# A list scheduler with transfer durations from a trace, later estimates for TensorE, and a second block handled by halves

## The chip, the core and the metric

The kernel runs on one core of a Trainium2 chip. A core has engines with instruction streams of their own: TensorE (PE; matmuls, and PEld for its weight loads), VectorE (DVE), ScalarE (ACT), GpSimd (POOL) and SyncE (SP). SP issues most of the transfers; sixteen DMA engines carry them. Each engine works off its own stream strictly in the order in which it was written, and waits on semaphores for the others. The metric is the device time of one execution in microseconds (us).

## What is computed

An attention with a decaying complex state, followed by a mixture of experts over all tokens:

```python
# B, H, S, D = 4, 8, 768, 48; per step t:
S_re, S_im = (ar * S_re - ai * S_im) + kv, ar * S_im + ai * S_re   # kv = k_t v_t^T, a normalised to |a| < 1
y[:, :, t] = q_t . S_re
...
x = y as (3072, 384)
P = exp(x @ w_gate - max), then 8 rounds of normalising rows and columns
out = sum over 8 experts e of P[:, e] * (relu(x @ w1[e]) @ w2[e])   # w1[e]: 384x1024, w2[e]: 1024x384
```

Matmuls are done to fp32 accuracy with split operands: each operand is a high part (one rounding) and a low part (the rest), and a product takes three matmuls.

## The kernel before

**Two phases.** Phase 1 (`phase1`) does the attention for 12 blocks of 256 tokens, and beside it experts 0 and 1 on the blocks whose x is done. Phase 2 (`phase2a`, `phase2b`) does experts 2 to 7 on units of 768 tokens with a fast matrix multiplication scheme of 15 products; it ends with the mixing by P. The change touches phase 1 alone.

**A block i in phase 1** has 256 tokens in two chunks c of 128. Its steps, with the method that adds them:

- `load(i)`: SP brings qk (768 KB) and v (512 KB).
- `norm(i)`: z (the complex decay a, 768 KB) is brought, then a chain that goes to and fro between ScalarE (Square L403, root L405, Square L406 and L409) and VectorE (L404, L407, L408, L410, L411, two products L413).
- `scan(i)`: the running product of a inside the block, all on VectorE (L440 to L445).
- `post(i)`: reciprocal magnitudes (ScalarE L485, L487, L488; VectorE L486, L491 to L493), then kh = k scaled (L495) and z times q (L497).
- `attention(i)`, per chunk: 6 transfers "ks" and 6 "qs" turn kh and z to head-major tiles (L531, about 64 KB each, all issued by SP); TensorE transposes keys (L539), forms scores (L549, needs ks and qs), state update U (L560) and outputs yp (L574). VectorE masks the scores (L552) and updates the state (L603 to L608). ScalarE copies keys (L542), a few columns of qs (L578 to L580) and evicts yp as xh (L596); VectorE makes the low part xl (L597). x then goes to DRAM (L614).
- `logits(i)`: x times the gate (L627, L628, L632 on TensorE; L635, L637 on ScalarE).
- `experts(i - 1)`: for each of 2 experts and 8 slices, first matmul (L264 to L266), relus on ScalarE (L270, hh and hf), low part on VectorE (L274), second matmul (L282 to L284), at the end evictions (L290) and a transfer (L305).

`weights` prepares experts 0 and 1 at the start: a load (L217 whole, L237 in thirds), the high part on ScalarE (L220, L242), the low part through TensorE with an identity and a negated identity (L203, L204) and back by ScalarE (L207).

**Who sets the order.** None of this is put in order by hand. Each step calls `Plan.add(engine, us, run, reads, writes, rank, ...)`; `Plan.order` then plays a list scheduler: it keeps a clock per engine (PE, DVE, ACT, SP), takes the engine that can start first, and of that engine's ready operations the one with the lowest rank. The result is one fixed order of instructions for each engine. An operation is ready when all that it depends on has ended, plus a reach from one engine to the other:

```python
REACH = {("PE", "ACT"): 0.20, ("PE", "DVE"): 0.20, ("DVE", "DVE"): 0.11, ("ACT", "PE"): 0.35, ("DVE", "PE"): 0.35, ...}
...
wait = 0.12 if e == "DVE" else 0.0     # VectorE may hold on this long for a better rank
...
pipe = max(t + 0.3, pipe) + kb / 330.0     # a transfer: queued behind the others,
end = max(pipe, t + kb / 210.0) + 1.6      # and with a time of its own by its size
```

So the times in `add` are estimates that decide only the order. On the chip an engine whose next instruction has to wait stands still, even if a later one could run.

At the last step of the attention the plan is cut: expert operations that come after it (`rest`) are issued in phase 2a, beside the loading of phase 2's X tiles (L686 to L715).

**Ranks.** Block i's scan and post have ranks from 1000 i. The norm of block i + 1 has a rank just below the scan of block i (from i + 1 = 2 on), with its last three VectorE operations 900 later. Attention steps have large negative ranks (first when ready), expert matmuls 10 n.

Of the kernel before, what the change touches and what calls it, by code (L numbers as in the profile page):

```python
# [18 lines left out]
CH = 128  # L19
# [36 lines left out]


class Plan:
    REACH = {("PE", "ACT"): 0.20, ("PE", "DVE"): 0.20, ("DVE", "DVE"): 0.11, ("ACT", "PE"): 0.35, ("DVE", "PE"): 0.35, ("ACT", "ACT"): 0.12, ("PE", "PE"): 0.0, ("SP", "PE"): 0.3}

    def __init__(self):
        self.ops, self.wrote, self.read = [], {}, {}

    def add(self, eng, us, run, reads=(), writes=(), rank=0, kb=0, late=0.0, after=()):
        deps = set(after)
        for r in reads:
            deps |= self.wrote.get(r, set())
        for w in writes:
            deps |= self.wrote.get(w, set()) | self.read.get(w, set())
        k = len(self.ops)  # L70
        self.ops.append((eng, us, run, rank, kb, late, sorted(deps)))
        for w in writes:
            self.wrote[w], self.read[w] = {k}, set()
        for r in reads:
            if r not in writes:
                self.read.setdefault(r, set()).add(k)
        return k

    def order(self):
# [10 lines left out]
        pipe = 0.0  # L90
        for k in range(n):
            if not left[k]:
                queue[self.ops[k][0]].append(k)
        out = []
        while any(queue.values()):
            best = None
            for e, q in queue.items():
                if q:
                    t = max(free[e], min(ready[k] for k in q))
                    if best is None or t < best[0]:  # L100
                        best = (t, e)
            t, e = best
            wait = 0.12 if e == "DVE" else 0.0
            k = min((k for k in queue[e] if ready[k] <= t + wait), key=lambda k: (self.ops[k][3], k))
            queue[e].remove(k)
            eng, us, run, rank, kb, late, deps = self.ops[k]
            t = max(t, ready[k])
            self.start[k] = t
            free[e] = t + us
            end = t + us  # L110
            if kb:
                pipe = max(t + 0.3, pipe) + kb / 330.0
                end = max(pipe, t + kb / 210.0) + 1.6
            self.end[k] = end
            out.append(k)
            for u in users[k]:
                r = end + (0.1 if kb else self.REACH.get((e, self.ops[u][0]), 0.15))
                ready[u] = max(ready[u], r)
                left[u] -= 1
                if not left[u]:  # L120
                    queue[self.ops[u][0]].append(u)
        assert len(out) == n
        return out


class Net:
# [63 lines left out]
    def weights(self, wx):  # L190
# [18 lines left out]
        for n in range(RING):  # L209
            e, f = divmod(n, NF)  # L210
            s = ("wx", n % 4)

            def load(n=n, e=e, f=f):
                assert len(raws) == n
                self.wt[e, f] = (self.wp if n < WIDE else self.wy).tile([128, 2, 2 * C], F32R, tag="w", name=f"w{e}_{f}")
                raws[n] = wx.tile([128, 2 * C], F32, tag="w", name=f"wr{e}_{f}")
                nc.sync.dma_start(raws[n], self.w[e, f])  # L217

            job("SP", 0.45, load, (), [s], -1.9e6 + 1e4 * n, kb=384)
            job("ACT", 0.74, lambda n=n, e=e, f=f: A.activation(self.wt[e, f][:, 0, :], raws[n], AF.Copy), [s], [("wh", n)], 10 * n)  # L220
            for j in range(2):
                cs = slice(j * C, j * C + C)
                piece_w(lambda n=n, cs=cs: raws[n][:, cs], lambda e=e, f=f: self.wt[e, f], cs, banks[turn % 4], [s, ("wh", n)], [("wl", n, j)], 10 * n + j, 0.65)
                turn += 1
            self.wd[e, f] = ([("wh", n), ("wl", n, 0)], [("wh", n), ("wl", n, 1)])
        thirds, k = {}, 0
        for n in range(RING, NF + N1):
            e, f = divmod(n, NF)
            for j in range(3):
# [15 lines left out]
                job("SP", 0.45, load, (), [s], -1.7e6 + k, kb=128)  # L245
# [8 lines left out]
    def experts(self, i):  # L254
# [37 lines left out]
        for e in range(2):  # L292
            for f in range(NF):
                n = (2 * i + e) * NF + f
                p = self.ph[n % 2][:, :SUB]
                b, q = ("ph", n % 2), (self.nthird + n) % (LAG + 1)
                w1, w2 = self.wd[e, f]
                job("PE", 1.07, lambda e=e, f=f, p=p: first(e, f, p), xr + w1, [b], 10 * n, late=0.0)
                job("ACT", 0.28, lambda e=e, f=f, p=p: relu("hh", e, f, p), [b], [("hh", q)], -1e6 + 2 * n)
                job("ACT", 0.28, lambda e=e, f=f, p=p: relu("hf", e, f, p), [b], [("hf", n % 2)], -1e6 + 2 * n + 1)  # L300
                job("DVE", 0.345, lambda e=e, f=f: low(e, f), [("hh", q), ("hf", n % 2)], [("hl", q)], -1e6 + n)
                job("PE", 1.05, lambda e=e, f=f: second(e, f), [("hh", q), ("hl", q)] + w2, [("po", 0), ("po", 1)], 10 * n + 5)
            for k in range(NCH):
                job("ACT", 0.5, lambda e=e, k=k: evict(e, k), [("po", k)], [("yst", k)], -8e5)
                job("SP", 0.45, lambda e=e, k=k: nc.sync.dma_start(self.ye_d[e][i * NCH + k], Y[e, k]), [("yst", k)], (), 0, kb=192)  # L305
        self.expert.update(range(n0, len(self.plan.ops)))

    def phase1(self, c1, ca):
# [65 lines left out]

    def load(self, i):
        nc, job, qk, vt = self.nc, self.plan.add, self.qk, self.vt
        job("SP", 0.45, lambda: nc.sync.dma_start(qk, self.aqk[i, :, 2:4]), (), [("qk", c) for c in range(NCH)], -1.85e6 if i == 0 else -1e5, kb=768)
        job("SP", 0.45, lambda: nc.sync.dma_start(vt, self.v[i]), (), ["v"], -1.65e6 if i == 0 else -1e5, kb=512)

    def norm(self, i):  # L380
        nc, V, A, job = self.nc, self.nc.vector, self.nc.scalar, self.plan.add
# [3 lines left out]
        R = 1000 * i  # L385
        if i == 0:
            for a in range(2):
                job("SP" if a else "ACT", 0.45, lambda a=a: (nc.sync if a else nc.scalar).dma_start(zt[:, a, :, :CH], self.aqk[0, :, a]), (), [("z", s, a, c) for c in range(NCH)], -2e6, kb=384)
        else:
            job("SP", 0.45, lambda: nc.sync.dma_start(zt[:, :, :, :CH], self.aqk[i, :, 0:2]), (), zn, -1.82e6 if i == 1 else -1e5, kb=768)  # L390
        for ps in ([[0], [1]] if i == 0 else [[0, 1]]):
            def nm(*t):
                return [(*t, c) for c in ps]
# [4 lines left out]
            zs = [("z", s, a, c) for a in range(2) for c in ps]  # L398
            X, Y, Z, Q = nm("tx"), nm("ty"), nm("tz"), nm("sq")
            f0, f1 = (i, ns + i) if ps[0] == 0 else (2 * ns + ns * NCT * NCH, 2 * ns + ns * NCT * NCH + 1)  # L400
            r = R - 1001 + ps[0] / 2 if i > 1 else R - 300 + 20 * ps[0]
            u = 900 if i > 1 else 0
            job("ACT", n / 522 + 0.1, lambda z=z, sq=sq, f0=f0: A.activation(sq, z, AF.Square, accum_out=fl[:, f0:f0 + 1]), zs, Q, r - 5e5)  # L403
            job("DVE", n / 960 + 0.105, lambda sq=sq, x=x: V.scalar_tensor_tensor(x, sq[:, 0], 1e-20, sq[:, 1], ALU.max, ALU.add), Q, X, r)  # L404
            job("ACT", n / 1045, lambda x=x, y=y: A.activation(y, x, AF.Abs_reciprocal_sqrt), X, Y, r + 1 - 5e5)  # L405
# [64 lines left out]
    def post(self, i):  # L470
# [1 line left out]
        s, fl, ns = i % 2, self.fl, self.N // SUB  # L472
        zt, G = self.zt[s], NCT * NCH
        xs, gs = (t.rearrange("p a g t -> p (a g t)").rearrange("p (g t) -> p g t", t=CH) for t in (self.ta, self.tb))
        for ps in ([[0], [1]] if i == 0 else [[0, 1]]):
            n = 3 * CH * len(ps)
            z, kh, qk = self.cut(zt[:, :, :, :CH], ps), self.cut(self.kh, ps), self.cut(self.qk, ps)
            x, g = (t[:, 3 * ps[0]:3 * ps[0] + 3 * len(ps)] for t in (xs, gs))
# [20 lines left out]
    def attention(self, i):  # L499
# [17 lines left out]
        def chunk(c):  # L517
# [9 lines left out]
            for t, dst, src, w in (("ks", ks, kh, CH), ("qs", qs, zt, CH + 1)):  # L527
                for a in range(2):
                    for ct in range(NCT):
                        p = 64 * a + 16 * ct  # L530
                        job("SP", 0.6, lambda p=p, dst=dst, src=src, w=w, a=a, ct=ct, c=c: nc.sync.dma_start(dst[p:p + 16, :, :w], src[:, a, ct * NCH + c, :w]),  # L531
                            [("kh", a, c)] if t == "ks" else [("z", s, a, c), ("ze", s, c)], [(t, ib, a, ct)], -3e6 + 20 * q + (6 if t == "qs" else 0) + 3 * a + ct, kb=170)
# [79 lines left out]
            chunk(c)  # L612
        for a, t in enumerate(("xh", "xl")):
            job("SP", 0.62, lambda a=a: nc.sync.dma_start(self.x_d[i // NS][:, i % NS, a], x_of()[a].bitcast(F32).rearrange("p c (j t) -> p c j t", t=CH)),  # L614
                [(t, s, c) for c in range(NCH)], (), -2e5, kb=384)

    def logits(self, i):
        nc, A, job = self.nc, self.nc.scalar, self.plan.add
# [737 lines left out]
```

## Time and profile before

| | us |
|---|---|
| median of 3 runs | 1784.88 (1783.31 to 1785.74) |
| profiled execution, its time | 1789.63 |
| profiled execution, its span | 1787.9 |
| TensorE busy in it | 1712.7 |
| VectorE busy | 1302.5 |
| ScalarE busy | 763.4 |
| granted TensorE clock, mean | 0.990 |

The page sums up one profiled execution. Rows by stage (a stretch of the span) give for each engine the busy time and the count of instructions, PE, PEld, DVE, ACT and POOL in this order, then the granted TensorE clock as a share of full speed, the mean busy share of the 16 DMA engines, and GB/s. Rows of waits read: who waited, for whom, us in total, times, longest. Rows in order of time begin with the start and the duration in us; in brackets stands the engine's idle time before, and who ended it. Rows of transfers give KB each and the median us from issue to landing.

### The profile page before, as it was taken

How to read it: one execution, taken by the hardware profiler on the slowest of the kernel's cores; microseconds unless marked ns; L12 is line 12 of the kernel's file. 1: busy time of each engine (PE TensorE's matmuls, PEld its weight loads, DVE VectorE, ACT ScalarE, POOL GpSimd, SP SyncE). 2: the span in 40 equal slices, each digit the busy share in tenths (PEclk: the TensorE clock that was granted, in tenths of full speed). 3: DMA queues.
4: the chain of work that ended last, by engine and by line, in shares of the span. 5: the costliest groups of instructions: out<-in, count | busy, mean ns of one | idle time of the engine just before them, and what ended most of it. 6: DMA issues, size and time to landing. Idle time of an engine off the chain costs nothing.

```text
span 1787.9 us, 32828 instructions
## 1 busy us (share of the span) xinstructions
PE 1712.7 (96%) x12696; PEld 1661.9 (93%) x12696; DVE 1302.5 (73%) x2892; ACT 763.4 (43%) x1694; POOL 6.4 (0%) x15
## 2 busy tenths in 40 slices
PE   6889999999999999999999999999999999999998
PEld 3878898888889898999999999999999999999998
DVE  7888888888888558999985567665566766556564
ACT  7544444444444354655553333333433333333332
POOL 1000000000000000000000000000000000000000
PEclk9999998999999999999999999999999999999999
DMA  6343332333333665787887465667555557455551
GB/s 205 106 119 119 111 95 67 114 109 106 116 118 93 194 235 198 261 292 271 292 305 272 176 234 189 248 226 252 224 187 220 202 218 261 183 223 179 224 227 45
DMA packets 180388, 335.90 MB, mean 188 GB/s; under 512 B 15104, under 2 KB 139776, under 8 KB 180224
## 3 DMA queue, kind: packets, MB, share of 16 engines
q1 hardware_dynamic: 179440, 333.33, 53.7%
q8 instruction: 102, 1.67, 0.4%
q14 instruction: 62, 0.51, 0.1%
q10 hardware_dynamic: 784, 0.39, 0.1%
HBM read 233.71 MB, written 81.00 MB: 176 GB/s over the span
## 4 chain that ended last, share of the span: by engine, by line


## 5 line engine op out<-in xcount | busy, mean ns | idle before, releaser
L1094 ACT ACTIVATE hh<-s 128x384 fp32r<-128x384 f32 x384 | 202.0, 526 | 424.5 <-DVE s L1090 383.9
L1090 DVE TENSOR_TENSOR s<-s,A 128x384 f32<-128x384 f32 x316 | 174.4, 552 | 145.2 <-PE A L1076 139.2
L1000 PE MATMUL po<-w_d,hl 128*128 128x384 f32 x768 | 256.6, 334 | 0.0
L999 PE MATMUL po<-w_d,hh 128*128 128x384 f32 x768 | 256.6, 334 | 0.0
L998 PE MATMUL po<-w_d,hh 128*128 128x384 f32 x768 | 256.6, 334 | 0.0
L1101 DVE SCALAR_TENSOR_TENSOR hl<-s,hh 128x384 fp32r<-128x384 f32 x384 | 211.8, 551 | 6.2
L264 PE MATMUL ph<-xh,w 128*128 128x256 f32 x576 | 166.1, 288 | 7.0 <-ACT hf L270 6.9
L265 PE MATMUL ph<-xl,w 128*128 128x256 f32 x576 | 163.0, 283 | 0.0
L266 PE MATMUL ph<-xh,w 128*128 128x256 f32 x576 | 163.0, 283 | 0.0
L270 ACT ACTIVATE hh<-ph 128x256 fp32r<-128x256 f32 x192 | 73.2, 381 | 176.6 <-PE ph L266 176.0
L1087 ACT ACTIVATE s<-B 128x384 f32<-128x384 f32 x192 | 94.3, 491 | 119.3 <-PE B L1076 115.8
L998 PEld LDWEIGHTS po<-w_d,hh 128*128 128x128 f32 x768 | 144.2, 188 | 0.0
L1000 PEld LDWEIGHTS po<-w_d,hl 128*128 128x128 f32 x768 | 144.1, 188 | 0.0
L999 PEld LDWEIGHTS po<-w_d,hh 128*128 128x128 f32 x768 | 144.1, 188 | 0.0
L1090 DVE TENSOR_TENSOR s<-s,B 128x384 f32<-128x384 f32 x189 | 104.0, 550 | 54.4 <-PE B L1076 52.0
L282 PE MATMUL po<-w,hh 128*128 128x384 f32 x384 | 134.6, 350 | 0.0
L284 PE MATMUL po<-w,hl 128*128 128x384 f32 x384 | 130.2, 339 | 2.4 <-DVE hl L274 2.3
L283 PE MATMUL po<-w,hh 128*128 128x384 f32 x384 | 129.4, 337 | 0.0
L1000 PE MATMUL po<-w_c,hl 128*128 128x384 f32 x384 | 128.5, 335 | 0.0
L999 PE MATMUL po<-w_c,hh 128*128 128x384 f32 x384 | 128.5, 335 | 0.0
L998 PE MATMUL po<-w_c,hh 128*128 128x384 f32 x384 | 128.5, 335 | 0.0
L1109 DVE TENSOR_TENSOR s<-s,B 128x384 f32<-128x384 f32 x64 | 35.5, 554 | 117.1 <-PE B L1076 116.1
(236 smaller groups left out, 4063.0 us busy)
## 6 DMA issues: line engine op xcount, KB each, us to landing
w_d<-w_d SPq DMA_DIRECT2D x64, 768.0 KB, 6.8
w_a<-w_d SPq DMA_DIRECT2D x48, 768.0 KB, 4.3
w_b<-w_d SPq DMA_DIRECT2D x48, 768.0 KB, 5.7
w_c<-w_d SPq DMA_DIRECT2D x48, 768.0 KB, 6.1
raw<-in_w_dram SPq DMA_DIRECT2D x32, 576.0 KB, 5.4
w_d<-w_a SPq DMA_DIRECT2D x16, 768.0 KB, 3.2
w_d<-w_b SPq DMA_DIRECT2D x16, 768.0 KB, 4.7
w_d<-w_c SPq DMA_DIRECT2D x16, 768.0 KB, 6.2
```

The lines of the kernel that those rows point to most:

```text
L264: nc.tensor.matmul(p, w[:, 0, cs], xh[:, ct, :], start=(ct == 0), stop=False)
L265: nc.tensor.matmul(p, w[:, 0, cs], xl[:, ct, :], start=False, stop=False)
L266: nc.tensor.matmul(p, w[:, 1, cs], xh[:, ct, :], start=False, stop=(ct == NCT - 1))
L282: nc.tensor.matmul(o, hh[:, s], w2h, start=f == 0, stop=False)
L283: nc.tensor.matmul(o, hh[:, s], w2l, start=False, stop=False)
L284: nc.tensor.matmul(o, hl[:, s], w2h, start=False, stop=f == NF - 1)
L998: nc.tensor.matmul(po[k], hh[:, s], w2[:, 0], start=c == 0, stop=False)
L999: nc.tensor.matmul(po[k], hh[:, s], w2[:, 1], start=False, stop=False)
L1000: nc.tensor.matmul(po[k], hl[:, s], w2[:, 0], start=False, stop=c == NF - 1)
L1090: V.tensor_tensor(S[nm], S[nm], ps, op)
L1094: A.activation(hh, S[nm], AF.Relu)
L1101: V.scalar_tensor_tensor(hl, S[nm], 0.0, hh.bitcast(F32), ALU.max, ALU.subtract)
```

## The change

- **Transfers.** `add` has `land` in place of `kb`: a fixed time from issue to landing for each kind of transfer. The common pipe of the transfers is gone from the model. A consumer on TensorE is ready 1.2 us after the landing, any other 0.2 us (before: 0.1 for all).
- **Reaches.** To TensorE from ScalarE 0.5 (before 0.35), from VectorE 0.6 (0.35); from TensorE to VectorE 0.4 (0.2); from ScalarE to VectorE 0.25 (before the default of 0.15).
- **Look-ahead.** The 0.12 us for which an engine may hold on for a better rank applied to every VectorE operation. Now it applies to candidates of rank 0 to 999 on any engine, and to no others.
- **Next norm.** The norm of block 2 gets rank 1599 (behind scan 1, ahead of post 1) in place of 999, its ScalarE operations the same less 500000, and its last three VectorE operations are no longer 900 later. Blocks 3 on stay as they were.
- **Second block by chunks.** `post` works in two halves for blocks 0 and 1 (before: block 0 alone).
- **A second issuing queue.** The 12 qs transfers of block 0 are issued by ScalarE (`QACT = 1`), all others by SP as before; an issue is planned at 0.64 us (0.6).

```diff
+QACT = 1
...
-    REACH = {("PE", "ACT"): 0.20, ("PE", "DVE"): 0.20, ("DVE", "DVE"): 0.11, ("ACT", "PE"): 0.35, ("DVE", "PE"): 0.35, ("ACT", "ACT"): 0.12, ("PE", "PE"): 0.0, ("SP", "PE"): 0.3}
+    REACH = {("PE", "ACT"): 0.2, ("PE", "DVE"): 0.4, ("DVE", "DVE"): 0.11, ("ACT", "PE"): 0.5, ("DVE", "PE"): 0.6, ("ACT", "ACT"): 0.12, ("ACT", "DVE"): 0.25, ("PE", "PE"): 0.0}
...
-            wait = 0.12 if e == "DVE" else 0.0
-            k = min((k for k in queue[e] if ready[k] <= t + wait), key=lambda k: (self.ops[k][3], k))
+            k = min((k for k in queue[e] if ready[k] <= t + (0.12 if 0 <= self.ops[k][3] < 1000 else 0.0)), key=lambda k: (self.ops[k][3], k))
...
-            end = t + us
-            if kb:
-                pipe = max(t + 0.3, pipe) + kb / 330.0
-                end = max(pipe, t + kb / 210.0) + 1.6
-            self.end[k] = end
+            self.end[k] = end = t + (land or us)
...
-                r = end + (0.1 if kb else self.REACH.get((e, self.ops[u][0]), 0.15))
+                r = end + ((1.2 if self.ops[u][0] == "PE" else 0.2) if land else self.REACH.get((e, self.ops[u][0]), 0.15))
...
# weights: whole, thirds; y of an expert; qk, v; z of block 0, z of the others; x
-kb=384  -kb=128  -kb=192  -kb=768  -kb=512  -kb=384  -kb=768  -kb=384
+land=3.8  +land=3.4  +land=2.0  +land=5.6  +land=4.8  +land=4.0  +land=8.5  +land=4.8
...
-            r = R - 1001 + ps[0] / 2 if i > 1 else R - 300 + 20 * ps[0]
-            u = 900 if i > 1 else 0
+            r = R - 1001 if i > 2 else R - 401 if i == 2 else R - 300 + 20 * ps[0]
+            u = 900 if i > 2 else 0
...
-        for ps in ([[0], [1]] if i == 0 else [[0, 1]]):
+        for ps in ([[0], [1]] if i < 2 else [[0, 1]]):
...
-                        job("SP", 0.6, lambda ...: nc.sync.dma_start(dst[p:p + 16, :, :w], ...), ..., kb=170)
+                        eng, queue = ("ACT", nc.scalar) if t == "qs" and i < QACT else ("SP", nc.sync)
+                        job(eng, 0.64, lambda ...: queue.dma_start(dst[p:p + 16, :, :w], ...), ..., land=2.7)
```

More of the change, by code (lines that the diff above doesn't have):

```diff
@@ L58, with add @@
 class Plan:
-    REACH = {("PE", "ACT"): 0.20, ("PE", "DVE"): 0.20, ("DVE", "DVE"): 0.11, ("ACT", "PE"): 0.35, ("DVE", "PE"): 0.35, ("ACT", "ACT"): 0.12, ("PE", "PE"): 0.0, ("SP", "PE"): 0.3}
+    REACH = {("PE", "ACT"): 0.2, ("PE", "DVE"): 0.4, ("DVE", "DVE"): 0.11, ("ACT", "PE"): 0.5, ("DVE", "PE"): 0.6, ("ACT", "ACT"): 0.12, ("ACT", "DVE"): 0.25, ("PE", "PE"): 0.0}
     def __init__(self):
         self.ops, self.wrote, self.read = [], {}, {}
-    def add(self, eng, us, run, reads=(), writes=(), rank=0, kb=0, late=0.0, after=()):
+    def add(self, eng, us, run, reads=(), writes=(), rank=0, land=0.0, after=()):
         deps = set(after)
@@ L70, in add @@
         k = len(self.ops)
-        self.ops.append((eng, us, run, rank, kb, late, sorted(deps)))
+        self.ops.append((eng, us, run, rank, land, sorted(deps)))
         for w in writes:
@@ L80, in order @@
         n = len(self.ops)
-        left = [len(o[6]) for o in self.ops]
+        left = [len(o[5]) for o in self.ops]
         users = [[] for _ in range(n)]
         for k, o in enumerate(self.ops):
-            for d in o[6]:
+            for d in o[5]:
                 users[d].append(k)
-        ready = [o[5] for o in self.ops]
+        ready = [0.0] * n
         self.start, self.end = [None] * n, [None] * n
@@ L89, in order @@
         queue = {e: [] for e in free}
-        pipe = 0.0
         for k in range(n):
@@ L102, in order @@
             t, e = best
-            wait = 0.12 if e == "DVE" else 0.0
-            k = min((k for k in queue[e] if ready[k] <= t + wait), key=lambda k: (self.ops[k][3], k))
+            k = min((k for k in queue[e] if ready[k] <= t + (0.12 if 0 <= self.ops[k][3] < 1000 else 0.0)), key=lambda k: (self.ops[k][3], k))
             queue[e].remove(k)
-            eng, us, run, rank, kb, late, deps = self.ops[k]
+            eng, us, run, rank, land, deps = self.ops[k]
             t = max(t, ready[k])
@@ L217, in load @@
                 nc.sync.dma_start(raws[n], self.w[e, f])
-            job("SP", 0.45, load, (), [s], -1.9e6 + 1e4 * n, kb=384)
+            job("SP", 0.45, load, (), [s], -1.9e6 + 1e4 * n, land=3.8)
             job("ACT", 0.74, lambda n=n, e=e, f=f: A.activation(self.wt[e, f][:, 0, :], raws[n], AF.Copy), [s], [("wh", n)], 10 * n)
@@ L244, in weights @@
                 wxs = ("wx", n % 4)
-                job("SP", 0.45, load, (), [s], -1.7e6 + k, kb=128)
+                job("SP", 0.45, load, (), [s], -1.7e6 + k, land=3.4)
                 job("ACT", 0.3, hi, [s] if j == 0 else [s, wxs], [("wh", n, j)] + ([wxs] if j == 0 else []), 10 * n + 2 * j)
@@ L297, in experts @@
                 w1, w2 = self.wd[e, f]
-                job("PE", 1.07, lambda e=e, f=f, p=p: first(e, f, p), xr + w1, [b], 10 * n, late=0.0)
+                job("PE", 1.07, lambda e=e, f=f, p=p: first(e, f, p), xr + w1, [b], 10 * n)
                 job("ACT", 0.28, lambda e=e, f=f, p=p: relu("hh", e, f, p), [b], [("hh", q)], -1e6 + 2 * n)
@@ L304, in experts @@
                 job("ACT", 0.5, lambda e=e, k=k: evict(e, k), [("po", k)], [("yst", k)], -8e5)
-                job("SP", 0.45, lambda e=e, k=k: nc.sync.dma_start(self.ye_d[e][i * NCH + k], Y[e, k]), [("yst", k)], (), 0, kb=192)
+                job("SP", 0.45, lambda e=e, k=k: nc.sync.dma_start(self.ye_d[e][i * NCH + k], Y[e, k]), [("yst", k)], (), 0, land=2.0)
         self.expert.update(range(n0, len(self.plan.ops)))
@@ L376, in load @@
         nc, job, qk, vt = self.nc, self.plan.add, self.qk, self.vt
-        job("SP", 0.45, lambda: nc.sync.dma_start(qk, self.aqk[i, :, 2:4]), (), [("qk", c) for c in range(NCH)], -1.85e6 if i == 0 else -1e5, kb=768)
-        job("SP", 0.45, lambda: nc.sync.dma_start(vt, self.v[i]), (), ["v"], -1.65e6 if i == 0 else -1e5, kb=512)
+        job("SP", 0.45, lambda: nc.sync.dma_start(qk, self.aqk[i, :, 2:4]), (), [("qk", c) for c in range(NCH)], -1.85e6 if i == 0 else -1e5, land=5.6)
+        job("SP", 0.45, lambda: nc.sync.dma_start(vt, self.v[i]), (), ["v"], -1.65e6 if i == 0 else -1e5, land=4.8)
     def norm(self, i):
@@ L387, in norm @@
             for a in range(2):
-                job("SP" if a else "ACT", 0.45, lambda a=a: (nc.sync if a else nc.scalar).dma_start(zt[:, a, :, :CH], self.aqk[0, :, a]), (), [("z", s, a, c) for c in range(NCH)], -2e6, kb=384)
+                job("SP" if a else "ACT", 0.45, lambda a=a: (nc.sync if a else nc.scalar).dma_start(zt[:, a, :, :CH], self.aqk[0, :, a]), (), [("z", s, a, c) for c in range(NCH)], -2e6, land=4.0)
         else:
-            job("SP", 0.45, lambda: nc.sync.dma_start(zt[:, :, :, :CH], self.aqk[i, :, 0:2]), (), zn, -1.82e6 if i == 1 else -1e5, kb=768)
+            job("SP", 0.45, lambda: nc.sync.dma_start(zt[:, :, :, :CH], self.aqk[i, :, 0:2]), (), zn, -1.82e6 if i == 1 else -1e5, land=8.5)
         for ps in ([[0], [1]] if i == 0 else [[0, 1]]):
@@ L530, in chunk @@
                         p = 64 * a + 16 * ct
-                        job("SP", 0.6, lambda p=p, dst=dst, src=src, w=w, a=a, ct=ct, c=c: nc.sync.dma_start(dst[p:p + 16, :, :w], src[:, a, ct * NCH + c, :w]),
-                            [("kh", a, c)] if t == "ks" else [("z", s, a, c), ("ze", s, c)], [(t, ib, a, ct)], -3e6 + 20 * q + (6 if t == "qs" else 0) + 3 * a + ct, kb=170)
+                        eng, queue = ("ACT", nc.scalar) if t == "qs" and i < QACT else ("SP", nc.sync)
+                        job(eng, 0.64, lambda p=p, dst=dst, src=src, w=w, a=a, ct=ct, c=c, queue=queue: queue.dma_start(dst[p:p + 16, :, :w], src[:, a, ct * NCH + c, :w]),
+                            [("kh", a, c)] if t == "ks" else [("z", s, a, c), ("ze", s, c)], [(t, ib, a, ct)], -3e6 + 20 * q + (6 if t == "qs" else 0) + 3 * a + ct, land=2.7)
             def keys(g):
@@ L614, in attention @@
             job("SP", 0.62, lambda a=a: nc.sync.dma_start(self.x_d[i // NS][:, i % NS, a], x_of()[a].bitcast(F32).rearrange("p c (j t) -> p c j t", t=CH)),
-                [(t, s, c) for c in range(NCH)], (), -2e5, kb=384)
+                [(t, s, c) for c in range(NCH)], (), -2e5, land=4.8)
     def logits(self, i):
```

## The prediction

> **What bounds the kernel now.** I read the page first, then the busy time by stage, then TensorE's waits stage by stage, then the rows around each large wait.
>
> ```profile
> span 1787.9 us, 32828 instructions
> PE 1712.7 (96%) x12696; PEld 1661.9 (93%) x12696; DVE 1302.5 (73%) x2892; ACT 763.4 (43%) x1694; POOL 6.4 (0%) x15
> 0.00:35.00 35.00, 23.48 (x72) 14.45 (x73) 23.68 (x71) 27.04 (x55) 6.43 (x15) 1.00 0.77 252
> 35.00:68.00 33.00, 21.61 (x315) 19.07 (x314) 28.60 (x57) 18.36 (x49) 0.00 (x0) 0.84 0.44 120
> 68.00:127.00 59.00, 51.95 (x575) 48.78 (x573) 50.60 (x126) 26.31 (x66) 0.00 (x0) 0.97 0.36 108
> 127.00:612.00 485.00, 453.58 (x5029) 427.71 (x5028) 404.19 (x926) 215.83 (x564) 0.00 (x0) 0.99 0.36 106
> 690.00:1788.00 1098.00, 1091.77 (x6271) 1085.18 (x6269) 747.32 (x1601) 434.57 (x863) 0.00 (x0) 1.00 0.62 227
> ```
>
> TensorE (PE, second column of the stage rows) is the bound: it is busy 1712.7 of 1787.9 us, and its work stays the same. So the change can only take away idle time and half-clock time of TensorE. From 690 us on there are 6 us of idle in 1098, and the change touches no code there. In the planned first phase the idle is 11.5 us before 35, 11.4 in 35 to 68 (block 0's attention), 7.1 in 68 to 127 (block 1), and 31.4 in 127 to 612 (blocks 2 to 11). Some 61 us before 612 is all there is to win, and half clock on top.
>
> Who ends the waits of blocks 2 to 11, TensorE's first, then two of ScalarE's:
>
> ```profile
> PE s L549 <- DMA qs<-z: 12.8, 14, 1.7
> PE ph L264 <- ACT hf L270: 5.3, 7, 1.7
> PE s L628 <- DVE xl L597: 4.3, 6, 0.8
> PE s L627 <- ACT xh L596: 3.1, 2, 2.5
> PE s L549 <- ACT rn L580: 1.2, 1, 1.2
> ACT sq L403 <- DMA z<-in_aqk_dram: 32.9, 8, 8.6
> ACT rn L580 <- DMA qs<-z: 22.7, 15, 2.9
> ```
>
> These are not waits for lack of work. Matmuls of the previous block's experts are there to run, but the order is fixed in advance and a score or logit matmul stands ahead of them before its data has come. Such waits come from durations that the planner has too short:
>
> ```profile
> qs<-z SPq DMA_DIRECT2D x144, 64.5 KB, 2.6
> z<-in_aqk_dram SPq DMA_DIRECT2D x11, 768.0 KB, 8.1
> ```
>
> The planner before gave z 768/210 + 1.6 = 5.3 us plus 0.1, and it takes 8.1. It gave qs 170/210 + 1.6 = 2.4 plus 0.1 for any consumer.
>
> **The change, part by part.**
>
> *Scores, keys, states.* TensorE now counts on 2.7 + 1.2 = 3.9 us from a qs or ks issue, 1.4 more than before, and six issues at 0.64 instead of 0.60 add 0.24. The longest of the DMA waits above is 1.7, so 1.6 us of slack covers nearly all of 12.8 + 1.2 = 14.0 us, as long as expert matmuls fill the slot. Experts of block 1 end together with x of block 2, those of block 5 end later than x of block 6:
>
> ```profile
> 173.69 0.55 DVE L597 TENSOR_TENSOR xl<-yp,xh 128x384 fp32r<-128x384 f32 x1
> 174.56 0.85 ACT L290 ACTIVATE yst<-po 128x384 f32<-128x384 f32 x2
> ...
> 372.94 0.55 DVE L597 TENSOR_TENSOR xl<-yp,xh 128x384 fp32r<-128x384 f32 x1
> 385.90 0.52 ACT L290 ACTIVATE yst<-po 128x384 f32<-128x384 f32 x1
> ```
>
> So the store of work is about 1 us at 174 and 13 us at 386. TensorE cannot run ahead by more than that unless x comes earlier too.
>
> *Norm on ScalarE.* The Square at L403 stands in ScalarE's queue until z lands, and the eviction of x stands behind it. The worst case:
>
> ```profile
> 269.10 1.48 ACT L403 ACTIVATE sq<-z 128x1536 f32<-128x1536 f32 x1 [8.61 <-DMA z<-in_aqk_dram]
> 270.58 0.47 ACT L596 ACTIVATE xh<-yp 128x384 fp32r<-128x384 f32 x1
> 271.10 0.39 PE L627 MATMUL s<-xh,wgs 128*16 128x256 f32 x1 [2.47 <-ACT xh L596]
> 270.00:281.00 11.00, 9.21 (x35) 8.17 (x36) 7.42 (x18) 5.82 (x15) 0.00 (x0) 0.53 0.18 73
> ```
>
> With 8.5 + 0.2 planned, 3.3 us later than before, ScalarE takes evictions and relus first. That takes 8 x 3.3 = 26 of the 32.9 us of blocked ScalarE, and with it most of the 3.1 (L627) and a part of the 5.3 (hf) and 4.3 (xl). The larger reaches to TensorE (0.5 from ScalarE, 0.6 from VectorE, 0.4 from TensorE to VectorE) help the same rows: xl gains 0.2 + 0.25, six times, 2.7.
>
> Of 14.0 + 12.7 = 26.7 us I could argue away 14.0 + 3.1 + 2.7 + 2 (of hf) = 22. I take 11, half: a new order puts its own errors in other places, and the small store of work up to block 5 bounds what can be used. Bounds: 4 and 20.
>
> *Clock.* In the last row above (270 to 281) the granted clock is 0.53 for 11 us; at full clock those matmuls take some 5 us less. That stretch began with waits of 2.47 and 0.69 us, both of the kinds mended. I take 5, bounds 0 and 7. The Trainium skill, page "TensorE: Matmul & The Clock Gate", section "What's actually happening", has the half rate come after at least one idle window of about 3.4 us. The stretch here follows waits that are shorter, so the trace disagrees; by the page's rule this term would be 0 and the sum 12.
>
> *Block 0 and 1 up to x of block 1.* Experts of block 0 are done long before x of block 1:
>
> ```profile
> 105.30 1.02 ACT L290 ACTIVATE yst<-po 128x384 f32<-128x384 f32 x2
> 122.43 0.55 DVE L597 TENSOR_TENSOR xl<-yp,xh 128x384 fp32r<-128x384 f32 x1
> ```
>
> From 106 to 123 TensorE has only block 1's attention. What is won earlier is lost there, unless that x comes earlier. So I count only what the change does to x of block 1. By chunks: from the first op of post to the first ks issue block 1 (whole) took 97.51 - 88.66 = 8.9 us, block 0 (in halves) 41.58 - 37.35 = 4.2. The 24 issues on SP follow without a break from there, so x comes 4.6 us earlier.
>
> ```profile
> 37.35 0.56 DVE L486 SCALAR_TENSOR_TENSOR ta<-kh 128x384 f32<-128x384 f32 x1
> 41.58 4.47 SPq L531 DMA_DIRECT2D ks<-kh  x6
> 41.89 1.02 DVE L497 TENSOR_TENSOR z<-z,qk 128x384 f32<-128x384 f32 x2
> 46.16 3.75 SPq L531 DMA_DIRECT2D qs<-z  x6
> 53.74 0.73 DVE L552 COPY_PREDICATED sc<-mask,s 128x512 f32<-128x512 uint8 x1 [1.44 <-PE s L549]
> 55.45 0.72 DVE L552 COPY_PREDICATED sc<-mask,s 128x512 f32<-128x512 uint8 x1 [0.98 <-PE s L549]
> 88.66 0.95 DVE L486 SCALAR_TENSOR_TENSOR ta<-kh 128x768 f32<-128x768 f32 x1
> 97.51 4.01 SPq L531 DMA_DIRECT2D ks<-kh  x6
> 46.00:52.00 6.00, 2.08 (x13) 1.65 (x11) 5.43 (x8) 3.47 (x10) 0.00 (x0) 1.00 0.42 102
> ```
>
> Halves cost VectorE 2 x 0.56 - 0.95 = 0.17 us for each of 8 instructions, 1.4 us, partly behind ks issues. Block 0's twelve qs issues go to ScalarE. There qs of chunk 0 can start at 42.9 instead of 46.16, and ks of chunk 1 need not wait for them on SP. The price is 12 x 0.63 = 7.5 us of ScalarE (SP's 3.75 for six), which is free for 2.5 us in 46 to 52 alone. The weights' evictions queued behind the first six come 3.8 us later, and TensorE's weight pieces move with them into its 3.9 us of idle in 46 to 52. Without that cover it is 3.8 us more idle, but still ahead of x of block 1. For x of block 1 only VectorE's two waits for scores count, 1.44 + 0.98 = 2.4. Together 4.6 + 2.4 = 7, bounds 2 and 9. The Trainium skill, page "DMA: Bandwidth & Descriptors", section "Issuing engines are not separate DMA queues", says that transfers started by several engines interleave on the same 16 DMA engines and that only issue time is saved, usually a small thing. Here the engines are 0.42 busy while SP issues, so issue time is what binds; if the rule's "small" held, the sum would be 2.4 less.
>
> *Loads at the start.* The planner before queued its loads behind each other (330 KB a us); now each lands a fixed time after its issue (wr 3.8 and 3.4, qk 5.6).
>
> ```profile
> 7.15 9.05 SPq L237 DMA_DIRECT2D wr<-in_w_dram  x8
> ```
>
> Eight issues planned at 0.45 each, 3.6 us in all, took 9.05, with the DMA engines 0.77 busy over the first 35 us. The new plan will count on weights too early, and ScalarE can stand in front of a weight while a root of block 0's norm waits behind it. Bounds: 0, and 5.4 (9.05 - 3.6). I take 3 lost.
>
> *VectorE's look-ahead.* The 0.12 us by which VectorE held on for a better instruction now holds for ranks 0 to 999 only, that is block 0 (and the weights and early experts on other engines). From block 1 on VectorE takes any ready instruction in the small gap after a dependent one. That fills gaps (a gain) and lets a 0.95 us instruction in ahead of post or of the state update (a loss). Bounds: 5 gained, 20 lost; I take 3 lost. The norm of block 2 goes behind scan 1, still ahead of post 1: nothing, bounds 1.9 either way (two instructions of 0.95).
>
> **Sum:** 11 + 5 + 7 - 3 - 3 = 17 us. The profiled execution took 1789.63 us (span 1787.9 and 1.7 around it), so 1772.6 like for like; the median of the runs shown is 1784.88, 4.75 less, and gives 1768.
>
> **Rivals.**
>
> *Nearly all stalls go*: 7 + 20 + 7 = 34. A cap stands against the whole of it: the second phase needs its X tiles. The rows are x of block 11, the last of the X tiles, and the evictions of block 11's two experts.
>
> ```profile
> 606.85 0.55 DVE L597 TENSOR_TENSOR xl<-yp,xh 128x384 fp32r<-128x384 f32 x1
> L715 DVE TENSOR_TENSOR X<-xs,X x11: 548/549/559, 616.5 to 637.3; 128x384 fp32r<-128x384 f32 x11
> 651.30 0.49 ACT L290 ACTIVATE yst<-po 128x384 f32<-128x384 f32 x1
> 667.25 1.02 ACT L290 ACTIVATE yst<-po 128x384 f32<-128x384 f32 x2 [0.99 <-PE po L284]
> ```
>
> The tiles are done 667.25 - 637.85 = 29.4 us ahead of the last expert. If the attention's end stays where it is, some 30 us is the most: 1755.
>
> *Short waits do not set the clock, and the second queue is worth nothing*: 17 - 5 - 2.4 = 9.6 us, 1775. What speaks for it: in 46 to 52 the clock stood at 1.00 beside 3.9 us of idle, and all issues end on the same engines. Both are what the two pages' rules would have.
>
> *No change*: the loads of the start cost 5.4, of the 7 for x of block 1 so 1.6 stay; VectorE's chain gets no faster, so that blocks 2 to 5 use up the store of 1 to 13 us and then starve (4 instead of 11); the look-ahead costs its 3, the clock gives nothing: 1.6 + 4 - 3 = 2.6, 1782.
>
> *Slower*: VectorE without look-ahead. From x of block 2 (173.69) to x of block 11 a block takes 48.1 us. If five low-ranked instructions of 0.95 us a block get in between the dependent ones of post and of the state update, x comes every 52.9 us. An expert takes 16 us (651 to 667), so block 11's two must begin at 635 to end as now. With x of block 2 at 170 (7 earlier, 3 lost at the start), x of block 11 comes at 170 + 9 x 52.9 = 646, 11 us too late: 1795. It decides from (635 - 170) / 9 = 51.7, that is 3.6 us a block. Against it: VectorE is busy 404 of 485 us there, and has some 8 us a block in hand.
>
> **How the numbers follow.** Forecast (1760 to 1773) 0.50; clock and queue give nothing, 1775: 0.13; nearly all, 1755: 0.15; no change, 1782: 0.11; slower, 1795: 0.11. A measurement of this kernel can tell about 0.2%, 3.6 us. Faster takes the first three, 0.78; the fourth is within 0.2%, 0.11; slower 0.11. The range leaves out most of the slower case and the far end of "nearly all": 1752 to 1786.
>
> **What would show it.** Right: TensorE's idle in 127 to 612 falls from 31.4 to about 20; L549's wait for qs falls under 5 us; ScalarE's L403 wait for z falls under 10; no 10 us stretch at half clock; x of block 1 near 117; qs issues of block 0 under ScalarE's queue, beginning near 43. Wrong: a root of block 0's norm behind a weight load before 20 us; x of block 2 later than 174; new waits of L264 or L282 for weights.

## The result: 1.7% faster, and where the time went

| | before | after |
|---|---|---|
| median, us | 1785.31 (4 runs) | 1755.34 (4 runs) |
| span of the profiled execution, us | 1787.9 | 1753.7 |
| TensorE busy, us | 1712.7 | 1702.3 |

The ratio after to before is 0.9833, 95% interval 0.9816 to 0.9851. That is 30 us less; the prediction was 1768, 17 us less. The two profiled executions differ by 34.2 us, since the one before, at 1789.63 us, was 4.3 us above its kernel's median; so differences between the two profiles come out some 4 us too large in all.

The rows by stage of the profile after, in the same columns as those of before (the last row takes in blocks 2 to 11, as 127 to 612 did before; it ends 27 us after x of block 11, the row before 5 us after it):

```profile
0.00:35.00 35.00, 22.19 (x61) 12.68 (x62) 25.34 (x75) 24.23 (x48) 6.43 (x15) 0.90 0.76 252
35.00:68.00 33.00, 20.11 (x187) 16.60 (x185) 19.96 (x34) 19.01 (x53) 0.00 (x0) 0.74 0.67 113
68.00:127.00 59.00, 51.28 (x690) 48.58 (x689) 55.05 (x150) 25.76 (x70) 0.00 (x0) 1.00 0.32 93
127.00:600.00 473.00, 465.53 (x5174) 445.75 (x5175) 415.19 (x959) 226.30 (x596) 0.00 (x0) 1.00 0.41 120
```

Two things are to be seen. In blocks 2 to 11 TensorE's idle time fell from 31.4 to 7.5 us. In block 0 (35 to 68) it did not fall: 12.9 against 11.4, and VectorE's busy time there went from 28.6 to 20.0.

Two marks cut the span into three parts that hold the same work in both kernels: the low part of x of block 1, and the last evictions of phase 1. In the rows before these are 122.43 and 667.25. After:

```profile
127.13 0.55 DVE L593 TENSOR_TENSOR xl<-yp,xh 128x384 fp32r<-128x384 f32 x1
...
632.89 1.01 ACT L285 ACTIVATE yst<-po 128x384 f32<-128x384 f32 x2 [0.99 <-PE po L279]
```

So up to x of block 1 the new kernel is 4.7 us slower, from there to the end of phase 1 it is 39.1 us faster (505.8 against 544.8), and phase 2 takes as long as before (1787.9 - 667.25 = 1120.7 against 1753.7 - 632.89 = 1120.8).

The same middle part as a stage, from block 1's first expert matmul to the end of the last eviction, first before, then after:

```profile
123.60:668.30 544.70, 508.94 (x5407) 480.88 (x5406) 438.75 (x1007) 248.84 (x646) 0.00 (x0) 0.99 0.40 122
128.80:633.90 505.10, 498.37 (x5405) 478.38 (x5405) 432.67 (x999) 245.71 (x645) 0.00 (x0) 1.00 0.43 131
```

TensorE's idle time falls from 35.8 to 6.7 us, by 29, and its busy time by 10.6. Half clock explains between 5 and 6 of these 10.6: 10.2 and 3.4 us of it before, 2.4 after (127.8 to 131.2, of which 2.4 lie in the stage), each costing half its length. The rest of the busy time stays open.

The waits of blocks 2 to 11 after, TensorE's (behind a first row of 2.4 us for the relus' low parts), then ScalarE's two:

```profile
PE s L624 <- DVE xl L593: 2.1, 1, 2.1
PE s L545 <- DMA qs<-z: 1.7, 3, 0.9
PE ph L259 <- ACT hf L265: 1.3, 3, 0.5
PE s L545 <- ACT rn L576: 0.7, 1, 0.7
```

```profile
ACT rn L576 <- DMA qs<-z: 12.1, 11, 1.8
ACT sq L398 <- DMA z<-in_aqk_dram: 10.9, 6, 5.0
```

(Lines are 4 or 5 lower than before.) TensorE's wait for qs went from 12.8 us to 1.7, for relus from 5.3 to 1.3, and ScalarE's for z from 32.9 to 10.9. The wait for x's high part (3.1) is gone from the list.

### The profile page after: what moved, and what is told of

The parts are those of the page before. It is cut to its first block, busy times and chain, and to the rows that moved or that the text cites. A ratio compares the mean times of both kernels' runs of the same rounds, so it can differ in the third digit from the quotient of the medians.

```text
span 1753.7 us, 32852 instructions
## 1 busy us (share of the span) xinstructions
PE 1702.3 (97%) x12696; PEld 1658.3 (95%) x12696; DVE 1297.6 (74%) x2900; ACT 760.2 (43%) x1699; POOL 6.4 (0%) x15
## 4 chain that ended last, share of the span: by engine, by line
## 5 line engine op out<-in xcount | busy, mean ns | idle before, releaser
L277 PE MATMUL po<-w,hh 128*128 128x384 f32 x384 | 133.7, 348 | 0.0
```

The lines of the kernel that those rows point to most:

```text
L277: nc.tensor.matmul(o, hh[:, s], w2h, start=f == 0, stop=False)
```

## The experiments

All ratios are to the old kernel, measured on the same chip in the same job. Its median lay between 1788.75 and 1790.13 there, some 4 us above that of the first job, so ratios are compared, and a ratio times 1785.3 gives the us of the expectations. The runs come from several jobs on two chips, so where two ratios are compared, both intervals count. Every edit leads to a new order of all engines: what a run measures is that order, and the waits named are what moved with it in the traces. Where a time within phase 1 is given, it is from the profile of that run.

### What carries blocks 2 to 11

**z planned to land soon** (undo):

```diff
-... zn, -1.82e6 if i == 1 else -1e5, land=8.5)
+... zn, -1.82e6 if i == 1 else -1e5, land=5.2)
```

> The new kernel with one number changed: the load of z is planned to take 5.2 us (with 0.2 on top the 5.4 of before) and not 8.5. Theory A (each kind of mended duration carries its own waits): ScalarE again stands at the norm's Square while z lands (wait for z in blocks 2 to 11 from 10.9 back towards 30 us), evictions of x and relus come late behind it, TensorE's idle of blocks 2 to 11 rises by 6 to 12 us: 1762 to 1768. Rival B (one pad covers for another: the slack of TensorE's other operations hides a late ScalarE): ScalarE waits the same 30 us, but TensorE does not: within 3 us of 1755. Rival C (the looser look-ahead of VectorE carries the gain): also within 3 us.

Measured: 0.9976 (0.9964 to 0.9988), that is 1781: 25 us of the 30 are gone with one number. The edit takes in z of block 1 too: in the profile x of block 1 comes at 133.7, 6.6 us later than in the change, and the part behind it takes 19.7 us longer (659.17 - 133.7 = 525.5 against 505.8). ScalarE's wait and TensorE's waits, blocks 2 to 11 of this run:

```profile
ACT sq L398 <- DMA z<-in_aqk_dram: 53.5, 9, 8.3
```

```profile
PE s L623 <- ACT xh L592: 9.3, 4, 5.7
PE ph L259 <- ACT hf L265: 5.7, 8, 1.9
PE s L624 <- DVE xl L593: 4.0, 5, 1.3
...
PE s L545 <- DMA qs<-z: 0.3, 1, 0.3
```

Theory A holds in kind, but its 7 to 13 us were half or less of what was lost. Rivals B and C fall: ScalarE's 53.5 us did reach TensorE, through x's high part (9.3), the relus (5.7) and x's low part (4.0), while the score waits stayed away. In order of time one case looks like this (ScalarE; the Square waits 8.26 us, and an eviction of x comes after it):

```profile
224.28 1.48 ACT L398 ACTIVATE sq<-z 128x1536 f32<-128x1536 f32 x1 [8.26 <-DMA z<-in_aqk_dram]
...
226.29 0.49 ACT L592 ACTIVATE xh<-yp 128x384 fp32r<-128x384 f32 x1
```

**z alone, in the old kernel** (do one part alone):

```diff
# in Plan.order, a transfer with land set ends at t + land
-... zn, -1.82e6 if i == 1 else -1e5, kb=768)
+... zn, -1.82e6 if i == 1 else -1e5, kb=768, land=8.5 if i > 1 else 0.0)
```

> The old kernel with one thing changed: z of blocks 2 to 11 is planned to land 8.5 us after its issue (and 0.1), not by the pipe (5.3). Theory A (ScalarE in front of z is the largest single loss, 25 us when put back into the new kernel, 20 of them in blocks 1 to 11): 12 to 20 us faster than before, ratio 0.989 to 0.993, ScalarE's wait for z in blocks 2 to 11 from 32.9 to under 12 us. Rival G (with the old margins TensorE's other waits take its place): ScalarE's wait falls as much, the time by under 8 us, ratio above 0.9955.

Measured: 0.9868 (0.9845 to 0.9891), 24 us faster, more than theory A had it. Rival G falls. The first row is ScalarE's, the second TensorE's, both of blocks 2 to 11:

```profile
ACT sq L403 <- DMA z<-in_aqk_dram: 3.7, 4, 1.5
```

```profile
PE s L549 <- DMA qs<-z: 12.7, 14, 1.5
```

The score waits are all still there (12.7 against 12.8), and yet most of the gain is made. So most of what blocks 2 to 11 lost came from ScalarE's place in front of z, and not from them. x of block 11 comes at 583.1, 23.8 us earlier than before.

**ks and qs planned to land soon** (undo):

```diff
-r = end + ((1.2 if self.ops[u][0] == "PE" else 0.2) if land else ...)
+r = end + (0.2 if land else ...)
-... land=2.7)   # ks and qs
+... land=2.3)
```

> The new kernel with the transfers' consumers planned as before: 0.2 us after landing for TensorE too (not 1.2), qs and ks landing after 2.3 us (not 2.7), so 2.5 us in all as before. Theory A: TensorE stands at the scores again, 12 to 16 us more idle in blocks 2 to 11 with the line of the scores in front: 1767 to 1772. Rival B (other pads are enough): under 5 us, below 1760. Rival C: no difference, within 3 us of 1755.

Measured: 0.9877 (0.9857 to 0.9897), 8 us of the gain lost, between theory A and its rivals. The edit also takes the margin from the weights and other loads that TensorE reads. The waits for the heads' transfers in the same stage sum to 11.2 us; in the change there were 1.7 and 0.7 of the first two kinds and none of the third:

```profile
PE s L545 <- DMA qs<-z: 4.7, 5, 1.3
PE s L545 <- ACT rn L576: 4.1, 2, 2.3
PE s L535 <- DMA ks<-kh: 2.4, 3, 1.1
```

**Reaches as before** (undo; REACH of the old kernel):

> The new kernel with the reaches between engines as before (0.35 to TensorE, 0.2 to VectorE). Theory A: only the waits for xl, xh and relus come back, 3 to 8 us: 1758 to 1763. Rival B: none come back, within 3 us of 1755. Rival D (the reaches carry most, since every block has dozens of such hand-overs and only a few transfers): 15 us or more, 1770 up.

Measured: 0.9834 (0.9811 to 0.9857), no difference that can be told. In its profile phase 1 from x of block 1 on takes some 6 us longer than in that of the change (638.1 - 127.3 against 633.9 - 128.8, first expert matmul of block 1 to last eviction), but that is not seen in the runs' ratio. Rival D falls; A's lower end and B are not told apart.

**Look-ahead for all of VectorE** (undo):

```diff
-ready[k] <= t + (0.12 if 0 <= self.ops[k][3] < 1000 else 0.0)
+ready[k] <= t + (0.12 if e == "DVE" else 0.0)
```

> The new kernel with VectorE's look-ahead of 0.12 us for all its operations, as before. My prediction put the loss of that look-ahead at 3 us, so undoing it should give 1752. Rival C (without look-ahead VectorE fills the gaps after dependent operations and its chain gets faster, which lets x come earlier and keeps TensorE supplied): undoing it costs 8 us or more, 1763 up, with x of block 11 later by as much.

Measured: 0.9865 (0.9848 to 0.9883), 6 us slower, where my prediction had it 3 us faster; the interval just touches that of the change (0.9816 to 0.9851). The edit also takes the look-ahead from the other engines' operations of rank 0 to 999. x of block 11 comes at 584.8 in place of 572.8. This speaks for rival C's sign, with a size a little under its own. That gaps on VectorE are filled was not shown: its busy time and its number of records do not separate the two kernels cleanly.

**The transfers alone** (reaches, look-ahead, ranks, pieces and queue as in the old kernel):

> The old kernel with the transfers' durations and margins alone (land, 1.2 and 0.2, issues at 0.64); reaches, look-ahead, ranks, pieces and queues as before. Theory A with the losses measured by undoing (z 25 us, heads' transfers 8, look-ahead 6, reaches about 0): transfers alone give 24 us, ratio 0.986 to 0.988. Rival G (the parts only work together): under 12 us, ratio above 0.993.

Measured: 0.9832 (0.9804 to 0.9861), the whole gain of the change and slightly above theory A. All other edits together are worth nothing that can be told. They are not idle, though: the look-ahead wins some 6 us, and the next runs show what takes it away. The new rank of block 2's norm and the transfers of the heads in the old kernel were not tried by themselves.

### What was lost up to x of block 1

Block 0 in the profile of the change, in order of time (start, length, engine): the issues of both queues, TensorE's scores, and ScalarE and VectorE behind the issues; then the stretch 44 to 56 in the columns of the stages; last the third and fourth issue rows of SP before.

```profile
43.96 10.96 SPq L527 DMA_DIRECT2D ks<-kh  x12
45.22 11.35 ACTq L527 DMA_DIRECT2D qs<-z  x12
...
54.06 3.75 PE L545 MATMUL s<-qs,ks 112*128 112x128 f32 x16 [8.88 <-DMA qs<-z]
...
57.31 0.94 ACT L404 ACTIVATE tz<-ty,bm 128x768 f32<-128x768 f32 x1
...
58.55 0.93 DVE L406 SCALAR_TENSOR_TENSOR tx<-tz,tx 128x768 f32<-128x768 f32 x1
```

```profile
44.00:56.00 12.00, 3.12 (x12) 2.55 (x13) 7.22 (x13) 1.44 (x5) 0.00 (x0) 0.50 1.00 112
```

```profile
50.01 3.76 SPq L531 DMA_DIRECT2D ks<-kh  x6
53.88 3.79 SPq L531 DMA_DIRECT2D qs<-z  x6
```

Both queues issue side by side, and issuing the 24 transfers still takes 12.6 us (43.96 to 56.57). Before it took 16.1 (41.58 to 57.67; the 15.4 in the next expectation is too low). The DMA engines are now 1.00 busy, at 112 GB/s; with one queue they were 0.42 busy at 102. By the packet records, a packet of some 512 bytes took 32 ns before; here it took 69 on SP's queue and 73 on ScalarE's. The 0.42 did not mean that the rest was free. The price was on ScalarE: from 45.22 to 56.57 it can do nothing else, and a Square of block 1's norm that VectorE needs (L404, then L406) comes at 57.31. With one queue (the next run) it comes 8.1 us earlier.

**One queue** (undo): `QACT = 0`.

> The new kernel with all qs transfers of block 0 issued by SP again. In the profile of the change two queues at once kept the DMA engines 1.00 busy at 112 GB/s (one queue: 0.42 at 102), 24 issues took 12.6 us (15.4 before), and ScalarE, which issued for 11.4 us, held back a root of block 1's norm. Theory E (the second queue gains nothing for block 1's x and blocks ScalarE): undoing it gives 0 to 4 us, 1751 to 1755, with x of block 1 at 123 to 127. Rival F (the 2.8 us of issue time do count): undoing it costs 2 to 3 us, 1757 to 1758, x of block 1 at 129 to 130.

Measured: 0.9771 (0.9747 to 0.9794). That is 11 us faster than the change; its interval lies below that of the change. x of block 1 comes at 117.5, 9.6 us before that of the change and 4.9 before the old kernel's:

```profile
49.17 0.94 ACT L404 ACTIVATE tz<-ty,bm 128x768 f32<-128x768 f32 x1 [0.35 <-DVE ty L403]
```

```profile
44.00:56.00 12.00, 7.11 (x33) 6.27 (x33) 10.22 (x17) 5.93 (x18) 0.00 (x0) 0.78 0.38 94
```

```profile
117.51 0.55 DVE L593 TENSOR_TENSOR xl<-yp,xh 128x384 fp32r<-128x384 f32 x1
...
625.67 1.02 ACT L285 ACTIVATE yst<-po 128x384 f32<-128x384 f32 x2 [0.99 <-PE po L279]
```

VectorE and ScalarE are busy in the same 12 us for 10.2 and 5.9 us, against 7.2 and 1.4. Rival F falls; E holds and was too small.

**Two queues on the kernel with the transfers alone** (`QACT = 1` in the run above that had 0.9832):

> The kernel with the transfers' durations alone (0.9832), with the one addition that block 0's qs transfers are issued by ScalarE. Theory E (two queues fill the DMA engines with packets that take twice as long, and ScalarE cannot evict or do a root for 11 us): 5 to 11 us slower, ratio 0.986 to 0.990, DMA engines 0.9 busy or more around 50 us. Rival: the loss belongs to the rest of the new plan alone: within 0.002 of 0.983.

Measured: 0.9865 (0.9850 to 0.9880), 6 us slower; the intervals of the two overlap by a little. x of block 1 goes from 124.8 to 129.8, and the stretch around 50 us shows the same picture, so the second queue loses time there without the rest of the new plan:

```profile
46.00:58.00 12.00, 2.93 (x14) 2.80 (x14) 6.93 (x12) 0.63 (x3) 0.00 (x0) 0.50 1.12 119
```

The second queue in the old kernel itself was not tried.

**Post of block 1 whole** (undo; `if i == 0` in place of `if i < 2`):

> The new kernel with post of block 1 in one piece. My prediction put the halves at 4.6 us for x of block 1: undoing them should bring x of block 1 from 127 to 131 or 132, the time to 1759 or 1760. Rival: block 1's x is held by other things (block 0 being late, ScalarE, SP's issues), and the eight instructions more on VectorE cancel the rest: within 2 us of 1755.

Measured: 0.9819 (0.9796 to 0.9841), no loss, x of block 1 at 125.5. And with one queue:

> One issuing queue, and post of block 1 in one piece. With two queues undoing the halves changed nothing that could be told (0.9819 against 0.9833). Theory: the halves are worth nothing: ratio within 0.002 of 0.977. Rival: with the second queue gone the halves' 4.6 us on the way to x of block 1 come through: x of block 1 at 121 to 122 in place of 117.5, ratio 0.979 to 0.980.

Measured: 0.9780 (0.9767 to 0.9793) against 0.9771, x of block 1 at 119.3 against 117.5. The halves bring 1.8 us at that place and nothing that can be told in the time. In the change the first half does not run through as in block 0: from the first op of post to the first ks issue it took 102.34 - 95.37 = 7.0 us (8.9 whole, 4.2 in block 0), since experts' low parts and ScalarE's roots lie in between.

**Loads of the start as slow as they are** (with one queue):

```diff
-job("SP", 0.45, load, (), [s], -1.9e6 + 1e4 * n, land=3.8)
+job("SP", 0.45, load, (), [s], -1.9e6 + 1e4 * n, land=5.8)
-job("SP", 0.45, load, (), [s], -1.7e6 + k, land=3.4)
+job("SP", 1.2 if k < 8 else 0.45, load, (), [s], -1.7e6 + k, land=5.0)
```

> The new kernel with one issuing queue (ratio 0.977 so far), and with the loads of the start planned as slow as they are: weights landing after 5.8 us (3.8), thirds after 5.0 (3.4), the first eight thirds with 1.2 us of SP each (0.45; they took 9.6 us together). Theory H (planned too early, weights stand in ScalarE's queue ahead of block 0's norm and post; VectorE stood 2.9 us before post 0): post 0 begins 1 to 3 us earlier, x of block 1 at 115 to 117, ratio 0.9755 to 0.9765. Rival: the start is bound by the DMA engines (0.76 busy over 35 us) and any order waits as long: 0.977 to 0.979.

Measured: 0.9755 (0.9739 to 0.9771), not to be told from one queue alone (0.9771). In the profile of the change the mechanism can be seen. VectorE's scan of block 0 ends at 33.65 (33.31 + 0.34), 2.8 us earlier than before, yet post's first operation on ScalarE (L480) begins at 38.84, where it was 36.48 before. ScalarE works through the weights until then, and VectorE waits 5.22 us:

```profile
33.31 0.34 DVE L440 TENSOR_TENSOR z<-ta,tb 128x186 f32<-128x186 f32 x1
...
38.84 1.61 ACT L480 ACTIVATE kh<-z 128x768 f32<-128x768 f32 x2
...
39.74 0.56 DVE L481 SCALAR_TENSOR_TENSOR ta<-kh 128x384 f32<-128x384 f32 x1 [5.22 <-ACT kh L480]
```

With the slow loads the scan ends at 33.16 and L480 follows at 33.20: theory H is right about the start, and the gain is lost later. Rows of that run: post 0's first ScalarE op (37.11 with one queue alone), x of block 1 (117.51), x of block 8 (431.34) and the last evictions (625.67):

```profile
33.20 1.58 ACT L480 ACTIVATE kh<-z 128x768 f32<-128x768 f32 x2
...
113.92 0.55 DVE L593 TENSOR_TENSOR xl<-yp,xh 128x384 fp32r<-128x384 f32 x1
...
431.26 0.55 DVE L593 TENSOR_TENSOR xl<-yp,xh 128x384 fp32r<-128x384 f32 x1
...
625.09 1.01 ACT L285 ACTIVATE yst<-po 128x384 f32<-128x384 f32 x2 [1.00 <-PE po L279]
```

Post 0 starts 3.9 us earlier and x of block 1 comes 3.6 earlier, yet x of block 8 comes at the same time. TensorE gives the 3.6 us back between blocks 3 and 8, partly in two waits for qs (2.0 us together) that the other run does not have. What sets x of block 8 in both runs stays open.

**z planned later still** (with one queue; `land=10.0`):

> One issuing queue, and z of blocks 1 to 11 planned to land after 10 us and not 8.5. In the profile of the change ScalarE still waited 10.9 us for z in blocks 2 to 11. Theory: the plan is past the step, since TensorE has hardly a wait of that kind left (6.7 us of idle from block 1 on): within 0.002 of 0.977. Rival: more of the same helps again, 3 us or more, under 0.9755.

Measured: 0.9796 (0.9779 to 0.9812) against 0.9771 (0.9747 to 0.9794). The rival falls: more of the same does not help. The theory's own band (0.975 to 0.979) is just missed; whether it harms the intervals do not say. In the profile x of block 1 comes 2.7 us later (120.2), and the part from there to the last evictions takes about as long (509.0 against 508.2). ScalarE's wait for z falls to 1.5 us in blocks 2 to 11, and its wait for x's result (57.9 us, 20 times) is now the large one, but TensorE's list has no wait for x.

All four versions of the new kernel with one queue beat both kernels: their intervals lie below that of the change. The lowest are one queue alone (0.9771) and one queue with the slow loads (0.9755), which cannot be told apart.

## Why the prediction came out as it did

The forecast of a gain was right in sign, and 1755 lies in the range (1752 to 1786), but the size was 17 us for 30. The sum hides two misses of opposite sign: up to x of block 1 it had 4 us won (7 - 3) and 4.7 were lost, from there on it had 13 (11 + 5 - 3) and 39 were won. That the two came out near the forecast is partly luck. By its own terms:

- **Scores, keys, states; norm on ScalarE; clock** (11 + 5 = 16 us). The mechanism was right, the term was mis-sized: from x of block 1 to the end of phase 1 the gain was 39 us, 29 of it idle time of TensorE, for which I had 11 and at most 20. I had counted 22 us of waits that could be argued away and took half. Two steps of this failed. First, I put most of the weight on the scores (14.0 of 22) and 3 to 8 us on z; undoing z costs 25 us (some 20 of them behind x of block 1), undoing the transfers of the heads 8, and z alone, with all score waits left in place, wins 24. Second, I held that the small store of work (1 us at 174) bounds what TensorE can use "unless x comes earlier too". It did come earlier: ScalarE's Square stood in front of x's eviction itself. From x of block 2 to x of block 11 a block took 44.4 us (173.0 to 572.8) in place of 48.1, and 45.8 (170.7 to 583.1) with z alone in the old kernel. How far that pace sets the end stays open: with the transfers alone it was 46.2, at the same ratio as the change.
- **Clock.** The half-clock stretch of 270 to 281 is gone, and the mean of 127 to 600 rounds to 1.00, with 3.4 us at half clock left. At some 5 us this term fits for blocks 2 to 11. But a longer one came up in block 0, where TensorE waits 8.88 us for qs (before, block 0 had 6.8 and 3.4 us at half clock), so that the sign "no 10 us stretch at half clock" failed:

```profile
42.48:59.54 17.06, 6.92 (x27) 6.18 (x28) 10.99 (x20) 5.78 (x17) 0.00 (x0) 0.50 0.96 111
```

- **x of block 1** (7 us earlier): wrong sign, 4.7 later. The step that failed is the second queue: I took 0.42 busy DMA engines for free ones, and moved 7.5 us of issues to ScalarE, counting the weights' evictions behind them but not the next block's norm. They took 11.4 us, and a Square of that norm stood behind them. With one queue x of block 1 came 4.9 us earlier. The halves, for which I had 4.6, gave 1.8.
- **Loads at the start** (3 lost): right in engine and size (3.6 at x of block 1), shown by planning them slower. The step that was off is what stands behind the weights: it was the first operation of post 0, not a root of block 0's norm (whose last product ended at 16.9, before at 19.7). And the loss does not reach the end.
- **Look-ahead** (3 lost): wrong sign; by the undoing it wins some 6, with intervals that just touch. The slower rival built on it did not come.
- **Rivals.** "Nearly all stalls go" is what happened in blocks 2 to 11, though with a loss at the start that it did not have. That its 1755 is the measured number is luck: it comes from a cap, and the cap did not bind, as the attention's end moved along, from 606.85 to 572.8.
- **Signs.** TensorE's idle time (7.5 us in 127 to 600) and its wait for qs (1.7) passed their marks, and x of block 2 (173.0) stayed within its own. ScalarE's wait for z (10.9 for under 10) just missed, x of block 1 (127.1 for 117) missed by far, and the qs issues began at 45.2 for 43.
- **The two pages.** For the Trainium skill, page "DMA: Bandwidth & Descriptors", section "Issuing engines are not separate DMA queues", the trace agrees: transfers of two queues share the engines, 24 issues took 12.6 us in place of 16.1. The sum by that rule was nearer than mine in this term, and the cost on the issuing engine came on top. For the Trainium skill, page "TensorE: Matmul & The Clock Gate", section "What's actually happening", the trace does not agree as far as one idle window of 3.4 us is needed: see the last section.

## What to carry to other kernels

In an order that is fixed in advance, the most expensive wrong estimate is the one whose consumer stands on a shared engine ahead of other engines' releases: look for the longest wait of an engine that is far from busy (ScalarE, 43%), and ask what is queued behind it. Waits of the bound engine itself (12.7 us for qs) can stay without costing as much. Before a second queue is given transfers of 512-byte pieces, compare GB/s and not the busy share of the DMA engines, and count what the issuing engine cannot do meanwhile.

## What the runs showed of the hardware

**Busy share of the DMA engines is no measure of what is free.** With packets of some 512 bytes from SBUF to SBUF, one queue gave 102 GB/s at a share of 0.42, two queues 112 to 119 GB/s at 1.00 and 1.12, and a packet's time went from 32 to some 70 ns. The median from issue to landing was 4.4 us on either queue in that stretch, against 2.6 with SP's alone.

**The clock can halve after waits of some 2 us.** In the profile of the change, TensorE waits 0.61 and 2.13 us, and the next stretch of 3.4 us is granted half the clock:

```profile
125.31 0.29 PE L623 MATMUL s<-xh,wgs 128*16 128x256 f32 x1 [0.61 <-ACT xh L592]
...
127.74 0.36 PE L624 MATMUL s<-xl,wgs 128*16 128x256 f32 x1 [2.13 <-DVE xl L593]
```

```profile
127.80:131.20 3.40, 3.40 (x17) 3.14 (x18) 3.32 (x8) 2.13 (x5) 0.00 (x0) 0.50 0.66 258
```

In the old kernel such a stretch of 3.4 us follows a single wait of 1.74 us (507.63 to 509.37, clock 0.50 from 509.7), while a wait of 1.79 us at 361 is followed by none. The length of a wait alone does not tell. In the change the clock goes to half or back at 42.48, 59.54, 127.81 and 131.22, whole multiples of 3.41 us apart, and TensorE's busy share in the step of 3.41 us just ahead tells more. Two steps of the old kernel (around 507 and 361), the step ahead of 127.8 in the change, and two steps over which one wait of 2.33 us is spread in the run with ks and qs soon:

```profile
506.28:509.69 3.41, 1.67 (x12) 1.38 (x11) 2.25 (x10) 1.85 (x6) 0.00 (x0) 1.00 0.80 247
359.51:362.92 3.41, 1.79 (x14) 1.47 (x12) 2.87 (x12) 1.78 (x5) 0.00 (x0) 1.00 0.48 80
124.40:127.81 3.41, 0.66 (x14) 0.20 (x7) 3.31 (x12) 0.49 (x1) 0.00 (x0) 1.00 1.13 346
386.90:390.31 3.41, 2.39 (x30) 1.87 (x22) 3.07 (x14) 1.90 (x5) 0.00 (x0) 1.00 0.25 63
390.31:393.72 3.41, 2.10 (x28) 2.01 (x32) 0.87 (x3) 0.96 (x3) 0.00 (x0) 1.00 0.85 253
```

Half clock follows the first (0.49 busy) and the third (0.20), and none of the others (0.53, 0.70, 0.62). The line is not sharp: a step of the change with 1.61 of 3.41 us busy (114.16 to 117.57, 0.47) is followed by full clock. So waits of about 2 us are enough at times, and a 3.4 us stretch at half clock costs some 1.7 us more than the wait itself.
